# Weight maxima taken from the seventh attention piece on, and five planner durations set to traced values, in a one-core attention and softplus FFN kernel

## The chip, the cores and the metric

The kernel runs on 1 core of one Trainium2 chip. The metric is the device time of one execution in microseconds (us). The kernel before takes 1098.19 us, the median of 3 runs (1097.35 to 1099.35).

Engine names below: PE is the matmul engine (PEld its weight loads), DVE the vector engine, ACT the scalar engine, POOL the GpSimd engine, SP the engine whose queue issues nearly all DMAs. Each engine executes its own instructions strictly in the order in which the program lists them, and waits on semaphores for the others.

## The reference

```python
# attention: B, H, S, D = 8, 8, 576, 64
scores = (q @ k.T) / sqrt(D)
cum    = cumsum(log(clip(f, 1e-4, 1)))
scores = where(causal, -1e9, scores + cum[:, None] - cum[None, :])
attn   = exp(scores - max(scores)); attn /= sum(attn) + 1e-9
x      = (attn @ v), heads side by side: 4608 tokens x 512
# FFN: w_in 512 x 2048, w_out 2048 x 512
h   = x @ w_in
out = (max(h, 0) + log1p(exp(-|h|))) @ w_out
```

All inputs and the output are float32; the weights arrive as 64-bit words and are rebuilt to float32 on the core.

## The kernel before, in words

**Pieces of attention.** The attention work is a list of 70 jobs, called pieces below and numbered n = 0, 1, ...: two quads (n = 0, 1) and four pairs (n = 2 to 5), which do parts of four or two heads of the first batch; eight rests (n = 6 to 13) and eight mixed ones (n = 14 to 21, second batch), and then 48 whole heads of the other six batches. `nfirst` is 6 and `nstart` is 14. A piece consists of scores (PE, tiles named `s<n>_...`), row minima of the negated scores (DVE, line 1095), exponentials with row sums (ACT, line 1123), a transposition of the weights, the product with v (PE, tiles `o<n>_...`) and the write into `x` (the batch's attention output). In pieces up to n = 21 the transposition is done on PE into banks called `b<n>_...` (lines 1265 and 1268), with copies out by ACT or DVE. In the 48 whole heads the weights are split into two fp16 halves in the buffer `cross` (high part by ACT, POOL or DVE at line 256 or 258, low part by DVE at line 1190) and a DMA transposes them; the product with v (line 1400) is then written to `x` by an ACT pass (line 1420, `shift`) and a DVE pass that adds the low half (line 1424, `put`).

**FFN.** Blocks of tokens go through `h` (up product), softplus and `acc` (down product). Blocks 0 and 1 use the float32 weights (lines 1524 and 1645). From block 2 on all operands are fp16 high and low parts, scaled by powers of two (lines 1543 and 1626). For these scales the kernel needs the largest magnitude of each quarter of `w_in` and of the whole of `w_out`.

**Maxima of the weights.** `load_w_in` and `load_w_out` load one of 32 pieces of 128x512 (DMA `sti`, `sto`; then ACT, DVE, POOL, ACT and DVE passes that rebuild float32). Right behind the load each calls `largest`, which adds one reduction: DVE's line 564 for `w_in` (16 of them); for `w_out` either an ACT pass at line 562 or DVE's line 564. When a quarter's four maxima are listed, the main loop calls `find_top` at the next piece: a reduction on DVE (line 582, `tops`), a transposition on PE (line 586, tile `top<g>`, which needs a PSUM bank), a DVE reduction (589), a PE matmul (593) and five small DVE passes (598 to 602). `split_w_in` and `split_w_out`, which make the fp16 weights, wait for that.

**What sets the order.** Nothing is ordered by hand. Every step is an `Op` with one or more possible engines, each with a duration in us and a bias (`On(engine, cost, bias, port)`), the ops that it needs, and the buffers that it takes. `Plan.run` is a list scheduler over a window of 700 ops: it repeatedly takes the op that can start first by these durations, on the engine on which it would end first, and appends its instructions to that engine's list. So the durations decide both the order on each engine and which engine does a step. For each kind of buffer there is a queue in the order in which the ops were added, and an op that is not marked `loose` can take a buffer only when it is first in that queue. The PSUM banks of attention (tag `att`, at most four, later three) are one such kind: scores and `find_top`'s transposition are loose, the transposition of the weights (`weights`, tiles `b`) is not. `plan.fill` adds dummy matmuls on PE (`fill`, line 1823) where the plan leaves PE more than 0.5 us without work, about one per 0.215 us of 70% of the gap; it is switched off with the first down product.

Of the kernel before, what the change touches and what calls it, by code (L numbers as in the profile page):

```python
# [39 lines left out]

W_FROM, W_EACH = 0, 3
S_FROM, S_EACH = 9, 4


class Op:
# [220 lines left out]
def tile_decay_attention_softplus_ffn(  # L266
# [159 lines left out]
    h_up, h_down = (  # L426
        cpool.tile([P, len(BLOCKS), NG], F32, name=x) for x in ("h_up", "h_down")
    )
    tops_left = []
    top_ops, top_set, out_set = {g: [] for g in range(NG + 1)}, {}, []  # L430
    BITS = 0x7F800000

# [231 lines left out]
    def load_w_in(i):  # L664
        def new():
            w_in32[i] = piece("woh", i + 1)
            return w_in32[i]

        cc, fq = i % NCC, i // NCC
        src = w_in[cc * P : (cc + 1) * P, fq * 512 : (fq + 1) * 512]  # L670
        w_in_ready[i] = load_f64(src, new, f"i{i}")
        largest(i, 0, w_in32, on_dve(512))

    def load_w_out(i):
        def new():
            w_out32[i] = piece("wol", i + 1)
            return w_out32[i]

        w_out_ready[i] = load_f64(w_out[i * P : (i + 1) * P], new, f"o{i}")
        largest(i, 1, w_out32, [on_act(DM, 0.19), on_dve(DM, bias=SPARE_BIAS)])  # L680

    def split_w_in(i):
        cc, fq = i % NCC, i // NCC
# [199 lines left out]
    def attention(job):  # L883
# [139 lines left out]
        def prepare():  # L1023
            def begin(e):
                nonlocal t, tb, qA, qB, kA, kB
                t = T[number % 2]
                tb = t.bitcast(F32)
                qA, qB, kA, kB = (t[:, i, :] for i in range(4))

            def decay_rows(e):  # L1030
                e.dma_start(out=tb[64:ST, 1::2, :], in_=aug_d[bh])

            def q_hi(e):
                copy(e, t[:, 0, :], st["q"])

            def q_hi2(e):
                e.dma_start(out=tb[0:64, 1, :], in_=tb[0:64, 0, :])

            def q_lo(e):
                e.tensor_sub(t[64:P, 0, :], st["q"][64:P], tb[64:P, 0, :])  # L1040

            def k_hi(e):
                copy(e, t[:, 2, :], st["k"])

            def k_lo(e):
                e.tensor_sub(t[0:64, 3, :], st["k"][0:64], tb[0:64, 2, :])

            if not mixed_:
                split_v()
            if number < nplain + 2:  # L1050
                set_rows(number % 2, T0_end[2 * (number % 2)] + T0_end[2 * (number % 2) + 1])
            start = add(NO_ENGINE, begin, after=T_set[number % 2], takes=("T",), lag=0.0)
            a = add_dma(decay_rows, 18, after=[start, decay_ready["rows"]])
            lo_on = On("DVE", 0.75, 0.0, True)
            q1 = add(casts(S), q_hi, after=[start, st["qk"]])
            q2 = add(lo_on, q_lo, after=[q1])
            q3 = add_dma(q_hi2, 144, after=[q1])
            k1 = add(casts(S), k_hi, after=[start, st["qk"]])
            k2 = add(lo_on, k_lo, after=[k1])
            give("raw", [q2, k2])  # L1060
            st["T"] = [a, q2, q3, k2]


        def stat_tile(ti):
# [12 lines left out]
            for i, (a, z, acc) in enumerate(pieces):  # L1077
                box = {}
                final = z == end

                def scores(e, box=box, a=a, z=z):
                    o = keep_bank(box, "bank", "att", f"s{n}_{ti}_{a}")[:, 0 : z - a]
                    box["o"] = o[0:n_q]
                    if plain:
                        e.matmul(  # L1085
                            o, part32(0, q0, q0 + P), part32(1, a, z), start=True, stop=not quad,
                        )
                        return
                    o = box["o"]
                    e.matmul(o, qA[:, q0:end], kA[:, a:z], start=True, stop=False)  # L1090
                    e.matmul(o, qB[0:ST, q0:end], kB[0:ST, a:z], start=False, stop=True)  # L1091

                def row_min(e, box=box, w=z - a, i=i, final=final):
                    right = MW - P + n_q if final else w
                    e.tensor_tensor_reduce(  # L1095
                        out=box["o"], in0=box["o"], in1=cmask[0:n_q, right - w : right],
                        scale=-0.125, scalar=m0 if i else 3.0e38, op0=ALU.add, op1=ALU.min,
                        accum_out=m1 if final else m0,
                    )

                def sums(e, box=box, h=heads[ti % len(heads)]):
                    c, (plus, minus) = cum[0][:, 0:P], (x[:, h : h + 1].to_broadcast([BH, P]) for x in eye8)
                    e.matmul(box["o"], c, plus, start=False, stop=False)
                    e.matmul(box["o"], minus, c, start=False, stop=True)

                on = on_pe32(z - a) if plain else on_pe(z - a, 2)
                o = add(on, scores, after=st["T"], takes=("att",), loose=True)
                if quad:
                    o = add(on_pe32(2 * P), sums, after=[o, decay_ready["quad"]] + eye8_set)
                    cum_used.append(o)  # L1110
                m = add(
                    On("DVE", 0.076 + (z - a) / 960), row_min, lag=0.2, after=[o] + mask_set + stat_set,
                    takes=("stat",) if ti == 0 and i == 0 else (),
                )
                st.setdefault("scores", []).append(o)
                st.setdefault("min", []).append(m)
                mins.append(m)
                todo.append((a, z, acc, box))
# [47 lines left out]
        def turn_tile(ti):  # L1166
# [17 lines left out]
            for w, (to1, to2), of in todo:  # L1184

                def first_part(e, to1=to1, of=of):
                    times(e, to1, of, f_)

                def second_part(e, to1=to1, to2=to2, of=of):
                    e.scalar_tensor_tensor(to2, of, f_, to1, ALU.mult, ALU.subtract)  # L1190

                a = add(scales(w), first_part, after=deps)
                st["split"].append(
                    add(On("DVE", 0.12 + w / 960, 0.0, True), second_part, after=[a])
                )
            if ti < nt - 1:
                return
# [189 lines left out]
        def output(gi):  # L1387
# [37 lines left out]

            needs = last + x_taken.get(b, [])
            takes = () if b in x_taken else ("x32",)
            c = add(on_act(w, 0.095, psum=True), shift, after=needs, takes=takes)
            d = add(On("DVE", 0.136 + w / 960), put, after=[c])
            x_taken.setdefault(b, [c])  # L1430
            puts = [d]
            wrote.setdefault(b, []).append((tok, tok + w, d))
# [394 lines left out]
    for n in range(len(jobs) + 1):  # L1827
        while tops_left and tops_left[0][0] < n:
            find_top(tops_left.pop(0)[1])
        number_of["n"] = n  # L1830
        cur, nxt = att[n], att[n + 1]

        def prep(n=n, nxt=nxt):
# [40 lines left out]
            credit = run_ffn(credit + share)  # L1874
        old = cur
        if n >= nstart:
            while tops_left:
                find_top(tops_left.pop(0)[1])
            while splits_left:
                split_w_in(splits_left.pop(0)[0])  # L1880
            while out_splits:
                out_splits.pop(0)()
# [45 lines left out]
```

## Time and profile before

| | |
|---|---|
| median of 3 runs | 1098.19 us |
| the profiled execution itself | 1096.39 us |
| span in its trace | 1094.4 us |
| PE busy | 1047.5 us (96%) |
| DVE busy | 884.7 us (81%) |
| ACT busy | 833.1 us (76%) |
| POOL busy | 336.7 us (31%) |
| mean granted PE clock | 0.994 of full speed |

All shares and times of the profile belong to the one profiled execution, which is 1.80 us below the median. Times in the timelines count from the start of the span. "Busy" of PE includes the dummy `fill` matmuls. In the timelines each float32 matmul on PE shows as two records.

### The profile page before, as it was taken

To read this page: it belongs to the slowest core of one execution; us is meant where nothing else is said; L and a number is where in the kernel's file an instruction comes from. 1 tells how busy PE (TensorE), PEld (TensorE's weight loads), DVE (VectorE), ACT (ScalarE), POOL (GpSimd) and SP (SyncE) were. 2 spreads that over 40 slices of the span, in tenths; PEclk is the share of its full clock that TensorE was granted. 3 is DMA by queue.
4 is the path that set the end of the run, shared out by engine and by line. 5 is a ranking of instruction groups with operands and counts; after the bars stand their busy time and mean duration, and the time that the engine had idled before them with its cause. 6 is when DMAs were issued, how large, how long until landed. Compare 5 with 4: busy or idle time off the path is not lost.

```text
span 1094.4 us, 19162 instructions
## 1 busy us (share of the span) xinstructions
PE 1047.5 (96%) x6315; PEld 639.5 (58%) x6315; DVE 884.7 (81%) x2274; ACT 833.1 (76%) x2008; POOL 336.7 (31%) x431
## 2 busy tenths in 40 slices
PE   8999999989999999989999999989999999999998
PEld 7677777766556454556655544546655545456554
DVE  6899998899788998998788998888878998763332
ACT  5899899978778877878778777777787877655554
POOL 3234123334224542434243442342332343100000
PEclk9999999989999999999999999999999999999999
DMA  8777424447646665556555565555453654311000
GB/s 259 223 214 243 114 75 122 117 122 183 150 112 145 149 175 137 142 132 163 130 133 144 130 159 142 125 140 151 99 138 95 154 130 97 72 37 40 20 1 29
DMA packets 229299, 140.69 MB, mean 129 GB/s; under 512 B 191648, under 2 KB 208320, under 8 KB 229200
## 3 DMA queue, kind: packets, MB, share of 16 engines
q1 hardware_dynamic: 229032, 139.32, 50.4%
q8 instruction: 50, 0.82, 0.3%
q14 instruction: 49, 0.40, 0.1%
q10 hardware_dynamic: 168, 0.15, 0.0%
HBM read 73.27 MB, written 10.62 MB: 77 GB/s over the span
## 4 chain that ended last, share of the span: by engine, by line
PE 42%; DVE 32%; ACT 13%; issue 6%; POOL 4%; DMA 3%; SPq 0%; DVEq 0%; POOLq 0%; ACTq 0%
PE h L1543 14%; PE acc L1626 13%; DVE cross L1190 9%; ACT p L1123 6%; DVE s L1095 5%; DVE e L1589 4%; PE h L1524 2%; DVE x L1424 2%; DVE gh L1600 2%; POOL cross L258 2%; PE b L1265 2%; PE o L1321 2%; PE s L1090 2%; PE s L1085 2%; ACT gh L256 1%
## 5 line engine op out<-in xcount | busy, mean ns | idle before, releaser
L1543 PE MATMUL h<-xh,wi 128*128 128x256 f16 (+2 forms) x1536 | 375.7, 320 | 13.8 <-ACT p L1123 8.1
L1626 PE MATMUL acc<-wo,gh 128*128 128x512 f16 x1632 | 383.7, 381 | 0.3 <-ACT gh L256 0.2
L1543 PEld LDWEIGHTS <-wi 128*128 128x128 f16 x2304 | 213.9, 99 | 142.7 <-issue 22.5
L1123 ACT ACTIVATE p<-s,negm 128x288 f32<-128x288 f32 (+7 forms) x384 | 183.1, 479 | 96.7 <-DVE negm L1095 91.8
L1626 PEld LDWEIGHTS <-gh 128*128 128x128 f16 x1632 | 152.3, 98 | 169.6 <-issue 5.8
L1543 PE MATMUL h<-xl,wi 128*128 128x256 f16 (+2 forms) x768 | 233.1, 319 | 4.1 <-DVE xl L1498 4.1
L1589 DVE SCALAR_TENSOR_TENSOR e<-e,x 128x512 f32<-128x512 f32 (+1 forms) x152 | 98.8, 650 | 102.3 <-ACT e L1577 102.0
L1190 DVE SCALAR_TENSOR_TENSOR cross<-p,rsum,cross 128x512 f16<-128x512 f32 (+4 forms) x288 | 169.9, 621 | 11.1 <-POOL cross L258 7.9
L258 POOL TENSOR_SCALAR cross<-p,rsum 128x64 f16<-128x64 f32 (+4 forms) x158 | 155.5, 1001 | 34.9 <-DVE rsum L1143 17.7
L262 POOL CAST T<-raw 128x576 fp32r<-128x576 f32 x74 | 58.8, 808 | 332.6 <-PE s L1090 314.1
L256 ACT ACTIVATE gh<-e,g_up 128x512 f16<-128x512 f32 (+1 forms) x149 | 100.5, 675 | 75.8 <-DVE e L1589 74.5
L1095 DVE CUSTOM_DVE_ANT_0 s<-s,cmask 128x288 f32<-128x288 f32 (+6 forms) x320 | 136.4, 435 | 13.9 <-PE s L1091 6.7
L1090 PE MATMUL s<-T 128*64 128x64 f32 x336 | 128.9, 393 | 15.6 <-DVE x L1424 11.7
L1574 ACT ACTIVATE e<-h,h_down 128x512 f32<-128x512 f32 (+1 forms) x152 | 96.7, 636 | 49.1 <-PE h L1543 48.3
L1600 DVE SCALAR_TENSOR_TENSOR gh<-e,g_up,gh 128x512 f16<-128x512 f32 (+1 forms) x152 | 106.4, 700 | 30.3 <-ACT gh L256 28.5
L1091 PE MATMUL s<-T 68*64 68x64 f32 x336 | 97.9, 296 | 0.0
L1581 ACT ACTIVATE x<-h,h_down 128x512 f32<-128x512 f32 (+1 forms) x152 | 96.8, 637 | 0.1
L1577 ACT ACTIVATE e<-e 128x512 f32<-128x512 f32 (+1 forms) x160 | 93.6, 585 | 0.1
L1090 PEld LDWEIGHTS s<-T 128*64 128x64 f32 x336 | 61.1, 182 | 40.9 <-DVE x L1424 14.2
L1400 PE MATMUL o<-cross,v 128*128 128x64 f16 (+4 forms) x528 | 79.8, 285 | 3.0 <-DVE x L1424 1.6
L1400 PEld LDWEIGHTS <-v 128*128 128x128 f16 x528 | 50.4, 98 | 45.5 <-issue 2.3
L1123 ACT ACTIVATION_READ_ACCUMULATOR p<-s,negm 128x1 f32 (+1 forms) x384 | 74.8, 195 | 0.0
(152 smaller groups left out, 1342.3 us busy)
## 6 DMA issues: line engine op xcount, KB each, us to landing
raw<-in_qkT SPq DMA_DIRECT2D x112, 288.0 KB
vr<-in_vR SPq DMA_DIRECT2D x64, 160.0 KB
out<-ob SPq DMA_DIRECT2D x35, 256.0 KB
sti<-in_w_in SPq DMA_DIRECT2D x16, 512.0 KB
sto<-in_w_out SPq DMA_DIRECT2D x16, 512.0 KB
T<-T SPq DMA_DIRECT2D x56, 144.0 KB
vp<-in_vR SPq DMA_DIRECT2D x24, 320.0 KB
T<-in_qkT SPq DMA_DIRECT2D x8, 288.0 KB
```

The lines of the kernel that those rows point to most:

```text
L256: e.activation(out, in_, AF.Copy, scale=by)
L258: e.tensor_scalar(out, in_, by, None, ALU.mult)
L1090: e.matmul(o, qA[:, q0:end], kA[:, a:z], start=True, stop=False)
L1091: e.matmul(o, qB[0:ST, q0:end], kB[0:ST, a:z], start=False, stop=True)
L1095: e.tensor_tensor_reduce(out=box["o"], in0=box["o"], in1=cmask[0:n_q, right - w : right], scale=-0.125, scalar=m0 if i else 3.0e38, op0=AL ...
L1123: e.activation(o, box["o"], AF.Exp, bias=m1, scale=-1.0, accum_out=acc)
L1190: e.scalar_tensor_tensor(to2, of, f_, to1, ALU.mult, ALU.subtract)
L1400: e.matmul(box["ps"][:, w - x.shape[-1] : w], st["v16"][:, c], x, start=i == 0, stop=i == len(todo) - 1,)
L1543: e.matmul(o, l, r, start=m == 0, stop=m == 11)
L1589: e.scalar_tensor_tensor(o, box["e"], LARGE, x, ALU.min, ALU.max)
L1600: e.scalar_tensor_tensor(box["l"], box["e"], up, box["h"], ALU.mult, ALU.subtract)
L1626: e.matmul(st["acc", tt], l, r[fc], start=first and m == 0, stop=last and m == 2,)
```

## The change

Two things are changed.

First, `load_w_in` and `load_w_out` no longer add the maximum at once. They put it into one of two lists (`sizes_left`), with the number of the piece at which it was put there. The main loop takes up to three (`M_EACH`) from each list at every piece from n = 6 (`nfirst`) on, if they were put there at an earlier piece; at the end of piece 14 and later the lists are emptied.

Second, five durations by which the scheduler plans are changed: the low parts of q and k (0.75 to 0.79), the row minimum (0.076 to 0.12 beside its length, with its lag from 0.2 to 0.16), the low part of the attention weights (0.12 to 0.19), `shift` (0.095 to 0.2) and `put` (0.136 to 0.19). What is computed stays the same.

```diff
+M_EACH = 3
...
-        largest(i, 0, w_in32, on_dve(512))
+        sizes_left[0].append((number_of["n"], lambda: largest(i, 0, w_in32, on_dve(512))))
...
-        largest(i, 1, w_out32, [on_act(DM, 0.19), on_dve(DM, bias=SPARE_BIAS)])
+        on = [on_act(DM, 0.19), on_dve(DM, bias=SPARE_BIAS)]
+        sizes_left[1].append((number_of["n"], lambda: largest(i, 1, w_out32, on)))
...
-            lo_on = On("DVE", 0.75, 0.0, True)
+            lo_on = On("DVE", 0.79, 0.0, True)
...
-                    On("DVE", 0.076 + (z - a) / 960), row_min, lag=0.2, after=[o] + mask_set + stat_set,
+                    On("DVE", 0.12 + (z - a) / 960), row_min, lag=0.16, after=[o] + mask_set + stat_set,
...
-                    add(On("DVE", 0.12 + w / 960, 0.0, True), second_part, after=[a])
+                    add(On("DVE", 0.19 + w / 960, 0.0, True), second_part, after=[a])
...
-            c = add(on_act(w, 0.095, psum=True), shift, after=needs, takes=takes)
-            d = add(On("DVE", 0.136 + w / 960), put, after=[c])
+            c = add(on_act(w, 0.2, psum=True), shift, after=needs, takes=takes)
+            d = add(On("DVE", 0.19 + w / 960), put, after=[c])
...
         number_of["n"] = n
+        if n >= nfirst:
+            for x in sizes_left:
+                for _ in range(M_EACH):
+                    if x and x[0][0] < n:
+                        x.pop(0)[1]()
...
         if n >= nstart:
+            for x in sizes_left:
+                while x:
+                    x.pop(0)[1]()
```

Since the scheduler places every instruction anew, the lists of all engines differ. Line numbers in the changed kernel are 1 or 2 higher up to line 1830, and 10 higher at the end.

On PE at the start of the program, in the kernel before, behind the scores of the pairs (`s2`, `s3`): the dummy matmuls, the transposition of the first maxima (`top0`), and only then the transpositions of the first quad's weights (`b0`).

```order
L1085 MATMUL s2_0_0_247<-T00_72 128x256 [waits DMAHW1_49,DMAHW0_49,Activation_49]
L1085 MATMUL s2_1_256_251<-T00_72 128x256 [waits Activation_49]
L1085 MATMUL s3_0_0_255<-T00_72 128x256 [waits Activation_49]
L1823 MATMUL fill_317<-cmask_74 128x128 x36
L586 MATMUL top0_354<-ident_66,tops_104 1x128 [waits DVE_49,Activation_49]
L1823 MATMUL fill_317<-cmask_74 128x128 x5
L593 MATMUL top0_354<-ident_66,top_row_105 128x1 [waits DVE_49]
L1265 MATMUL b0_0_376<-ident_66,p0_640_95 128x128 [waits Activation_49]
L1265 MATMUL b0_0_376<-ident_66,p0_640_95 128x128
L1268 MATMUL b0_0_376<-ident_66,cross_102 128x128
```

The same place on PE in the changed kernel:

```order
L1087 MATMUL s2_0_0_247<-T00_72 128x256 [waits DMAHW1_49,DMAHW0_49,Activation_49]
L1267 MATMUL b0_0_251<-ident_66,p0_640_95 128x128 [waits Activation_49]
L1267 MATMUL b0_0_251<-ident_66,p0_640_95 128x128
L1270 MATMUL b0_0_251<-ident_66,cross_102 128x128 [waits Activation_49]
L1267 MATMUL b0_1_257<-ident_66,p0_640_95 128x128 x2
L1270 MATMUL b0_1_257<-ident_66,cross_102 128x128 [waits DVE_49]
L1087 MATMUL s2_1_256_262<-T00_72 128x256
L1087 MATMUL s3_0_0_272<-T00_72 128x256 [waits Activation_49]
L1323 MATMUL o0_275<-cross_102,vr0_163 64x128 [waits DMAHW3_49,Activation_49]
L1323 MATMUL o0_275<-cross_102,vr0_163 64x128
```

The first quad's `b0` now follows the first score of piece 2, and neither `top0` nor a `fill` stands ahead of it. In all, the list of PE holds 43 `fill` before and 17 now; `top0` moves from row 31 of PE's list to row 159, behind the first up products.

On DVE at the same time, before: the rebuilding of the first pieces of `w_in` (`ti`, `woh`) with a maximum behind each (`sizes_w`), and `tops` behind the fourth.

```order
L1143 RECIPROCAL rsum1_88<-lsum1_80 128x4 [waits DVE_49]
L631 TENSOR_SCALAR ti0_260<-ti0_260 128x512 [waits Activation_49]
L648 SCALAR_TENSOR_TENSOR woh1_dt_float32_262<-ti0_260,woh1_dt_float32_262 128x512 [waits Activation_49,Pool_49]
L631 TENSOR_SCALAR ti1_273<-ti1_273 128x512 [waits Activation_49]
L564 TENSOR_REDUCE sizes_w_103<-woh1_dt_float32_262 128x1 [waits DVE_49]
L631 TENSOR_SCALAR ti2_280<-ti2_280 128x512 [waits Activation_49]
L648 SCALAR_TENSOR_TENSOR woh2_dt_float32_271<-ti1_273,woh2_dt_float32_271 128x512 [waits Activation_49,Pool_49]
L564 TENSOR_REDUCE sizes_w_103<-woh2_dt_float32_271 128x1 [waits DVE_49]
```

And in the changed kernel, behind the first row minimum of piece 2:

```order
L1139 SCALAR_TENSOR_TENSOR lsum1_80<-lsum1_80,part1_84 128x4 [waits Activation_49]
L263 COPY cross_102<-b0_1_257 128x384 [waits PE_49]
L1145 RECIPROCAL rsum1_88<-lsum1_80 128x4 [waits DVE_49]
L1097 ISA s2_1_256_262,negm2_77<-s2_1_256_262,cmask_74 128x256 [waits PE_49]
L1097 ISA negm2_77 128x1
L632 TENSOR_SCALAR ti0_269<-ti0_269 128x512 [waits Activation_49]
L1097 ISA s3_0_0_272,negm3_78<-s3_0_0_272,cmask_74 128x256 [waits PE_49]
L1097 ISA negm3_78 128x1
L1361 TENSOR_TENSOR x32_0_291<-o0_275,cross_102 128x128 [waits PE_49]
```

Attention steps stand between the rebuilding passes, and the maxima of the first quarter come later (rows 72 to 76 of DVE's list, with `tops` at row 108 instead of 52).

In the part with whole heads the order changes in many small places. One of them on PE: the scores of the third tile of piece 56 (`s56_2`), which before stand right behind the last product of piece 54 (`o54_1`) and wait for DVE.

```order
L1400 MATMUL o54_1_8467<-cross_102,v16_54_8034 128x192
L1400 LDWEIGHTS v16_54_8034
L1400 MATMUL o54_1_8467<-cross_102,v16_54_8034 128x64
L1090 MATMUL s56_2_0_8483<-T0_1223 128x320 [waits DVE_49]
L1091 MATMUL s56_2_0_8483<-T0_1223 128x320
L1543 LDWEIGHTS wi16_0_390
L1543 MATMUL h9_0_8447<-xh9_7236,wi16_0_390 128x256
```

In the changed kernel the same scores stand ahead of both products of piece 54, and behind `o54_1` come scores that wait for ACT:

```order
L1092 MATMUL s56_2_0_8419<-T0_1177 128x320 [waits Activation_49]
L1093 MATMUL s56_2_0_8419<-T0_1177 128x320
L1545 LDWEIGHTS wi16_0_720
L1545 MATMUL h9_0_8423<-xh9_7249,wi16_0_720 128x256 [waits Activation_49]
```

```order
L1402 MATMUL o54_1_8471<-cross_102,v16_54_8036 128x192
L1402 LDWEIGHTS v16_54_8036
L1402 MATMUL o54_1_8471<-cross_102,v16_54_8036 128x64
L1092 MATMUL s56_3_0_8487<-T0_1177 128x448 [waits Activation_49]
L1093 MATMUL s56_3_0_8487<-T0_1177 128x448
```

Over the whole program 74 score matmuls of line 1090 wait for DVE before and 71 now; of these, 18 before and 16 now have no other matmul between themselves and the last product with v. Steps with a choice of engine move too: high parts of 128x512 attention weights on DVE 11 to 2, on ACT 46 to 45, on POOL 39 to 49; high parts of v on DVE 8 to 9, on ACT 25 to 11, on POOL 15 to 28; maxima of `w_out` on ACT 16 to 11, on DVE 0 to 5.

## Rows read from the trace of the kernel before

**Rows 1.** Stretches of the whole run: length, busy time of each engine, clock, DMA
```profile
0.00:60.00 60.00, 53.63 (x372) 41.59 (x373) 46.98 (x147) 43.96 (x116) 19.01 (x48) 1.00 0.80 227
60.00:120.00 60.00, 60.00 (x406) 44.88 (x404) 56.23 (x153) 55.02 (x136) 20.97 (x23) 1.00 0.72 220
120.00:180.00 60.00, 59.30 (x428) 44.03 (x427) 57.24 (x162) 54.98 (x146) 13.68 (x15) 1.00 0.39 103
180.00:240.00 60.00, 55.18 (x410) 41.08 (x409) 50.95 (x166) 50.72 (x146) 19.59 (x25) 0.94 0.49 122
...
sum 1094.40, PE 1047.52 PEld 639.49 DVE 884.71 ACT 833.13 POOL 336.75; mean PE 58.20 PEld 35.53 DVE 49.15 ACT 46.28 POOL 18.71
```

**Rows 2.** Timeline of PE, 13 to 48 us: start, length, instruction, idle before
```profile
13.75 8.20 PE L1823 MATMUL fill<-cmask 128*128 128x128 f32 x72
24.37 0.27 PE L586 MATMUL top<-ident,tops 128*1 128x128 f32 x1 [2.42 <-DVE tops L582]
24.48 1.28 PE L1823 MATMUL fill<-cmask 128*128 128x128 f32 x10
...
25.99 0.44 PE L1265 MATMUL b<-ident,p 128*128 128x128 f32 x2
...
26.70 0.61 PE L1823 MATMUL fill<-cmask 128*128 128x128 f32 x4
...
32.13 1.95 PE L1524 MATMUL h<-x,woh_dt_float 128*128 128x128 f32 x16
...
43.19 0.44 PE L1321 MATMUL o<-cross,vr 128*64 128x128 f32 x4 [1.28 <-ACT cross L262]
```

**Rows 3.** Timelines of ACT, DVE and SP, 11 to 30 us
```profile
11.87 0.28 ACT L262 COPY cross<-rsum 128x128 f32<-128x128 f32 x1
...
12.00 0.22 DVE L262 COPY cross<-rsum 128x128 f32<-128x128 f32 x1
...
22.62 0.69 DVE L648 SCALAR_TENSOR_TENSOR woh_dt_float<-ti,woh_dt_float 128x512 uint32<-128x512 uint32 x1
23.34 0.69 DVE L564 TENSOR_REDUCE sizes_w<-woh_dt_float 128x1 f32<-128x512 f32 x1
...
29.47 0.54 SPq L959 DMA_DIRECT2D T<-in_qkT  x1
```

**Rows 4.** Waits over the whole run: who for whom, us in total, times, longest
```profile
PE s L1090 <- DVE x L1424: 11.7, 13, 2.4
...
DVE cross L1190 <- POOL cross L258: 7.9, 19, 1.1
...
PE h L1543 <- DVE x L1424: 4.5, 6, 1.7
...
PE o L1400 <- DVE x L1424: 1.6, 1, 1.6
```

**Rows 5.** Timeline of PE at piece 56's scores
```profile
739.24 0.42 PE L1090 MATMUL s<-T 128*128 128x320 f32 x1 [2.38 <-DVE x L1424]
```

**Rows 6.** Groups by line and shape: busy us, mean ns of one, idle before
```profile
L1190 DVE SCALAR_TENSOR_TENSOR cross<-p,rsum,cross 128x512 f16<-128x512 f32 x96 | 70.7, 747 | 0.3
...
L258 POOL TENSOR_SCALAR cross<-p,rsum 128x512 f16<-128x512 f32 x39 | 62.2, 1598 | 0.0
...
L1424 DVE SCALAR_TENSOR_TENSOR x<-o,v_down,x 64x512 f32<-64x512 f32 x48 | 35.8, 745 | 1.2 <-ACT x L1420 0.4
...
L1190 DVE SCALAR_TENSOR_TENSOR cross<-p,rsum,cross 64x64 f16<-64x64 f32 x48 | 32.4, 674 | 7.1 <-POOL cross L258 6.0 <-ACT cross L256 0.8
...
L258 POOL TENSOR_SCALAR v<-vr,v_up 128x320 f16<-128x320 f32 x15 | 21.9, 1462 | 10.2 <-PE o L1400 6.2 <-PE o L1321 3.7 <-DMA raw<-in_qkT 0.2
...
L1190 DVE SCALAR_TENSOR_TENSOR cross<-p,rsum,cross 128x64 f16<-128x64 f32 x48 | 16.7, 347 | 0.1
...
L564 DVE TENSOR_REDUCE sizes_w<-woh_dt_float 128x1 f32<-128x512 f32 x16 | 10.7, 675 | 0.1
...
L258 DVE TENSOR_SCALAR cross<-p,rsum 128x512 f16<-128x512 f32 x11 | 7.3, 666 | 0.1
```

More of the change, by code (lines that the diff above doesn't have):

```diff
@@ L428, in tile_decay_attention_softplus_ffn @@
     )
-    tops_left = []
+    tops_left, sizes_left = [], ([], [])
     top_ops, top_set, out_set = {g: [] for g in range(NG + 1)}, {}, []
```

## The prediction

> **What bounds the kernel now.** I read the table of stretches first. PE works 1047.5 of 1094.4 us, so at most 46.9 us of idle time can be had, and what is worth reading is where it lies [rows 1]. The first stretch of 60 us lacks 6.4 us, the next two together 0.7 us, the fourth 4.8 us, at a clock of 0.94. From 60 to 180 us PE is the bound, with DVE close behind (113.5 of 120 us). Later each stretch lacks a few us.
>
> Busy is not the same as useful: the timeline of PE shows dummy matmuls from 13.75 us on, 8.20 + 1.28 + 0.61 = 10.09 us of them, 86 records, so 43 matmuls of 0.235 us. Behind the first group PE stands for 2.42 us until DVE has the maxima of the first quarter of `w_in`, and only then, at 25.99 us, come the transpositions of the first quad [rows 2]. Their inputs had long been there: the copies of the row sums that they read end at 12.2 us [rows 3]. So from 13.75 to 25.99 us PE does nothing but two tiny matmuls of `top0`. The cause is the queue for attention's banks, in the planner: the transposition of the maxima was listed ahead of `b0`, takes a bank of the same kind, and `b0` isn't loose, so it could not be planned before it. The maxima in turn wait for four weights to land and be rebuilt, until 23.3 us and 0.69 us more for the last maximum [rows 3].
>
> In the part with whole heads, PE's own waits are for `put`, which frees a bank or finishes x: 11.7 + 4.5 + 1.6 = 17.8 us, 20 times [rows 4]. The one at 739.24 us is typical, 2.38 us in front of scores that stand right behind a product with v [rows 5].
>
> **The change part by part.** (a) The start. `top0` no longer stands in front of `b0`, since the maxima are listed only from piece 6 on. 26 of 43 dummy matmuls go, 26 x 0.235 = 6.1 us, and the wait of 2.42 us goes: 8.5 us [rows 2]. A second limit gives the same: the next thing that must come from memory is the first up product, at 32.13 us, and its last weight was rebuilt at 23.3 us, 8.8 us before [rows 2, 3]. What is late next are the copies out of `b`, which now come on DVE and ACT between rebuilding passes. The nearest row is the 1.28 us that a product with v waits for such a copy at 43.19 us [rows 2]. Four products with v now stand ahead of the first up product, so 0 to 5.1 us are given back; I take 1.5 us, near one such wait, since by the list there are other matmuls between most `b` and their `o`. Net -7.0 us, between -8.5 and -3.4 us. SP's queue moves along: its load at 29.47 us waited for a buffer that the scores of piece 3 free, and they now stand ahead of the first up product [rows 3].
>
> (b) What was taken out comes back later. 16 maxima of 0.675 us on DVE stay 16 [rows 6]; eight of them stood in the first 60 us; in DVE's list now four stand at rows 72 to 76 and the others from row 109 on, so up to 4 x 0.675 = 2.7 us move into the stretch up to 180 us. Five maxima of `w_out` go from ACT to DVE there, 3.4 us at the same duration. Together 6.1 us come to a stretch in which DVE has 6.5 us free [rows 1]. What hides them is that room, and that the fp16 weights aren't used before the float32 blocks are through. I take 0, with 6.1 us if the cover is gone. The loads come earlier by as much as PE does: 227 x 60 + 220 x 60 is 26.8 MB in 120 us, in 113 us it would be 237 GB/s. The DMA engines are busy 0.80 and 0.72 there [rows 1], so I count nothing.
>
> (c) The durations. `put` of 512 columns takes 0.745 us [rows 6] where the plan had 0.136 + 0.533 = 0.669 and now has 0.723; the low part of 512 takes 0.747 where it had 0.653 and has 0.723 [rows 6]. With the plan's DVE later, it puts other work where PE would wait. The lists show a small effect: of scores that wait for DVE, 18 stood with nothing between themselves and the product with v, and 16 do now. Of 17.8 us I take 2/18, -2.0 us [rows 4]; the bounds are 0 and one half, -8.9 us, if every such place becomes milder like the one of piece 56, which goes altogether.
>
> (d) The engines. Ten more high parts of 512 columns go to POOL, at 1.598 us instead of 0.666 on DVE, 0.93 us later each; DVE already waits 7.9 us for such parts [rows 4, 6]. By the share of 10 to 39 it is 2.0 us of DVE waits; a quarter of it on PE makes +0.5 us. The bounds are 0 and 9.3 us, each of the ten in full. The 13 more parts of v on POOL, 1.462 us each, are needed only at the product with v, about a piece later: 0 as long as POOL is busy a third of the time.
>
> Sum against the profiled execution: 1096.39 - 7.0 + 0 - 2.0 + 0.5 = 1087.9 us. The median of the runs lies 1.80 us above it, so 1089.7 us.
>
> A rule that speaks against (d): the low part of 64x64 takes 0.674 us on DVE where that of 128x64, with as many elements a row, takes 0.347 [rows 6]. The Trainium skill (SBUF — State Buffer, "Who interferes with whom") says that DVE and GpSimd share a pair of ports under an exclusive lock, so that a DVE pass with two SBUF inputs and a GpSimd pass block each other in full. These rows fit it, as one of these passes follows POOL's and the other mostly doesn't; by it all of POOL's added time would stop DVE, which is the second rival.
>
> **The rivals.** *Given back by 180 us.* DVE is nearly full from 60 to 180 us, and if the 6.1 us of (b) don't fit, or the loads hold the start back, PE's lead of 7.0 us melts to 0.9. With (c) and (d) at nothing that is 1096.39 - 0.9 + 1.8 = 1097.3 us. For it speaks DVE's 113.5 of 120 us, against it that PE, not DVE, was without a gap there [rows 1].
>
> *Slower: POOL holds DVE.* POOL gets 10 x 1.598 + 13 x 1.462 = 35.0 us of passes more, less what narrower ones leave it [rows 6]. If they hold DVE's passes, and with them `put` and the row minima, and a third of that reaches PE, 11.7 us come on top of (a): 1096.39 - 7.0 + 11.7 + 1.8 = 1102.9 us. It decides from 9.2 us on, a good quarter. For it: DVE waits for POOL 19 times; against it: the longest is 1.1 us, and DVE's own list gets shorter by 13 rows.
>
> *A better plan throughout.* If the waits for `put` halve, the sum is 1096.39 - 7.0 - 8.9 + 0.5 + 1.8 = 1082.8 us; with no new waits at the start 1081.3. For it: the durations corrected are those of just the passes that PE waits for. Against it: 16 of 18 places remain.
>
> *No effect.* The gap at the start reappears somewhere before the weights: 1098 us. Against it: the list itself has lost the 26 matmuls.
>
> **How the numbers follow.** Chances: the forecast 0.62, given back 0.15, slower by POOL 0.10, the better plan 0.10, no effect 0.03. The forecast's own range is 1081 to 1096 us, from the ends of (a) and (c) and 2 us of (d). The range 1079 to 1099 us takes in the first rival and the better plan and leaves out the slower one. A difference under 0.2%, 2.2 us, can't be told from none. Faster by more: 0.62 + 0.10 + 0.03 of the given-back case, 0.75. Within: 0.10 of that case and no effect, 0.13. Slower: 0.10 + 0.02, 0.12.
>
> **What would show it.** Right on (a): the first `b` at 13 us instead of 25.99, the first up product at about 24 us, and dummy matmuls of about 4 us in all. Wrong on (a): waits for copies of over 5 us before 60 us, or a clock below 1.00 in the first stretch. On (b): the stretches from 60 to 180 us should lack no more than 1 or 2 us of PE; over 5 us is the first rival. On (c): PE's waits for `put` at 14 to 18 us. On (d): DVE's wait for POOL's high parts at 8 to 11 us; over 15 us, with waits for `put` over 25 us, is the slower rival. The forecast is wrong as a whole if PE's idle time after 240 us changes by more than 8 us either way.

## The result, and the profile after

The changed kernel takes 1068.99 us, the median of 4 runs (1068.78 to 1069.77), against 1097.77 us (1097.18 to 1099.35) for the kernel before beside it: a ratio of 0.974, 95% interval 0.9725 to 0.9756. The profiled execution took 1069.17 us with a span of 1067.1 us. The gain of 28.8 us is more than three times the forecast, and the time lies 10 us below the range.

The stretches of the changed kernel, in the columns of [rows 1], with a fifth one up to 1050 us:

```profile
0.00:60.00 60.00, 55.77 (x380) 41.61 (x380) 48.08 (x153) 45.43 (x122) 19.93 (x48) 1.00 0.87 251
60.00:120.00 60.00, 58.23 (x361) 42.51 (x362) 55.67 (x144) 51.29 (x125) 18.18 (x23) 0.94 0.65 191
120.00:180.00 60.00, 59.50 (x423) 44.11 (x422) 58.07 (x165) 54.22 (x147) 17.55 (x15) 1.00 0.39 104
180.00:240.00 60.00, 54.51 (x396) 41.06 (x395) 52.27 (x170) 50.90 (x147) 16.97 (x24) 0.91 0.50 125
240.00:1050.00 810.00, 799.72 (x4643) 461.25 (x4642) 650.89 (x1626) 624.58 (x1455) 290.20 (x332) 1.00 0.50 123
```

The last stretch in the kernel before, which [rows 1] hold only in their sum:

```profile
240.00:1050.00 810.00, 779.01 (x4497) 447.54 (x4497) 661.08 (x1627) 606.61 (x1427) 263.50 (x321) 1.00 0.51 123
```

The first 240 us gain nothing: PE lacks 4.2 + 1.8 + 0.5 + 5.5 = 12.0 us where it lacked 11.9. From 240 to 1050 us it lacks 10.3 us where it lacked 31.0. That is 20.7 us of the 27.3 us of span, all in the part with whole heads, for which the forecast had 2.

The start on PE in the changed kernel, in the columns of [rows 2]:

```profile
13.21 0.38 PE L1267 MATMUL b<-ident,p 128*128 128x128 f32 x2
...
21.24 1.73 PE L1825 MATMUL fill<-cmask 128*128 128x128 f32 x14
...
24.47 3.84 PE L1526 MATMUL h<-x,woh_dt_float 128*128 128x128 f32 x32
...
61.64 1.26 PE L1087 MATMUL s<-T 66*128 66x320 f32 x2 [1.98 <-issue]
```

The first `b` comes at 13.21 us instead of 25.99 and the first up product at 24.47 instead of 32.13; dummy matmuls fall from 10.1 to 4.6 us. The scores of piece 8 start 9.9 us earlier than before. Those of piece 10 are 3.1 us ahead, those of piece 20 are 0.5 us late, and those of piece 32 0.6 us late; at piece 56 they are 13.9 us ahead and at piece 69 23.1.

PE's and DVE's waits in the changed kernel, which answer to [rows 4]:

```profile
PE h L1545 <- DVE x L1426: 3.7, 4, 1.8
PE s L1092 <- ACT p L1125: 3.4, 4, 1.7
PE h L1545 <- DVE xl L1500: 2.8, 3, 1.8
...
DVE cross L1192 <- POOL cross L259: 4.6, 11, 0.7
```

The wait of scores for `put`, 11.7 us in 13 places, is gone, that of products with v too, and that of `h` is 3.7 us instead of 4.5: 17.8 us became 3.7. DVE waits less for POOL's high parts, not more.

The place of [rows 5], piece 56, in the changed kernel's timelines, first PE:

```profile
719.41 0.49 PE L1092 MATMUL s<-T 128*128 128x320 f32 x1
...
721.22 0.22 PE L1402 MATMUL o<-cross,v 128*128 128x64 f16 x2
...
722.59 1.44 PE L1402 MATMUL o<-cross,v 128*128 128x512 f16 x9
723.86 0.45 PE L1092 MATMUL s<-T 128*128 128x448 f32 x1
```

and DVE:

```profile
722.88 0.28 DVE L1426 SCALAR_TENSOR_TENSOR x<-o,v_down,x 64x64 f32<-64x64 f32 x1
```

`put` starts 1.44 us after the end of the product that it follows (721.44 us), where the kernel before took 5.90 us (733.02 to 738.92, shown below). And the scores of 320 columns are through before that, so PE goes on without a gap.

Groups by shape of the changed kernel, against [rows 6]:

```profile
L1192 DVE SCALAR_TENSOR_TENSOR cross<-p,rsum,cross 128x512 f16<-128x512 f32 x96 | 70.9, 753 | 1.1 <-POOL cross L259 0.8
...
L259 POOL TENSOR_SCALAR cross<-p,rsum 128x512 f16<-128x512 f32 x49 | 82.0, 1675 | 0.0
...
L259 POOL TENSOR_SCALAR v<-vr,v_up 128x320 f16<-128x320 f32 x28 | 46.3, 1652 | 29.5 <-PE o L1402 28.0 <-PE o L1323 1.1 <-DMA raw<-in_qkT 0.4
```

### The profile page after: what moved, and what is told of

The parts are those of the page before. It is cut to its first block, busy times and chain, and to the rows that moved or that the text cites. A ratio compares the mean times of both kernels' runs of the same rounds, so it can differ in the third digit from the quotient of the medians.

```text
span 1067.1 us, 19053 instructions
## 1 busy us (share of the span) xinstructions
PE 1040.8 (98%) x6263; PEld 636.5 (60%) x6263; DVE 869.0 (81%) x2262; ACT 833.6 (78%) x2005; POOL 362.8 (34%) x441
## 4 chain that ended last, share of the span: by engine, by line
PE 66%; DVE 17%; ACT 6%; issue 4%; POOL 4%; DMA 2%; DVEq 0%; POOLq 0%; ACTq 0%
PE h L1545 24%; PE acc L1628 23%; PE o L1402 4%; DVE s L1097 3%; PE s L1092 3%; DVE cross L1192 3%; PE s L1093 2%; ACT p L1125 2%; PE h L1526 2%; DMA cross<-cross 2%; PE b L1267 2%; PE acc L1647 2%; POOL cross L259 2%; DVE e L1591 2%; PE s L1087 1%
## 5 line engine op out<-in xcount | busy, mean ns | idle before, releaser
L259 POOL TENSOR_SCALAR cross<-p,rsum 64x64 f16<-64x64 f32 (+4 forms) x157 | 164.1, 1061 | 36.2 <-DVE rsum L1145 15.1
L1192 DVE SCALAR_TENSOR_TENSOR cross<-p,rsum,cross 128x512 f16<-128x512 f32 (+4 forms) x288 | 161.7, 596 | 6.9 <-POOL cross L259 4.6
L263 POOL CAST T<-raw 128x576 fp32r<-128x576 f32 x73 | 53.6, 747 | 267.5 <-PE s L1092 228.5
L257 ACT ACTIVATE gh<-e,g_up 128x512 f16<-128x512 f32 (+1 forms) x144 | 97.0, 674 | 56.6 <-DVE e L1591 55.6
L1602 DVE SCALAR_TENSOR_TENSOR gh<-e,g_up,gh 128x512 f16<-128x512 f32 (+1 forms) x152 | 109.4, 719 | 30.2 <-ACT gh L257 29.4
```

What stands on the lines that cost most here:

```text
L259: e.tensor_scalar(out, in_, by, None, ALU.mult)
L1602: e.scalar_tensor_tensor(box["l"], box["e"], up, box["h"], ALU.mult, ALU.subtract)
```

## The experiments

Each run's time has beside it its ratio to the kernel before on the same chip, with the 95% interval. "Idle" is what PE lacks from 240 to 1050 us in the run's trace.

**Which half of the change.** e1 has the five durations alone, e2 the deferred maxima alone.

```diff
# e1: the five durations of the change; sizes_left and M_EACH are left as before
# e2: the change, with
-            d = add(On("DVE", 0.19 + w / 960), put, after=[c])
+            d = add(On("DVE", 0.136 + w / 960), put, after=[c])
# ... and the other four durations as before
```

> The kernel before with the five durations of the change, the maxima taken as pieces arrive. Theory D (the durations do it in the part with whole heads: PE's waits for `put` go because the plan no longer believes DVE to be free early): 1070 to 1078 us, PE's waits for `put` under 6 us in all, the start as before (first `b` at about 26 us). Theory M (the deferred maxima do it, by a head start that lasts): 1092 to 1098 us. Theory R (any new plan can fall this way): nothing said, somewhere from 1065 to 1100 us.

> The change with the five durations as before: only the maxima are deferred. Theory D: 1093 to 1098 us; the lead of about 10 us at 50 us is given back by 230 us, as in the changed kernel, and PE's waits for `put` stay at 14 to 18 us. Theory M: 1070 to 1080 us. Theory R: anywhere from 1065 to 1100 us, with the difference spread over the whole run.

e1: 1071.86 us (0.9782, 0.9744 to 0.982), idle 8.9 us. e2: 1096.25 us (0.9988, 0.9973 to 1.0004), idle 33.8 us. From piece 44 on every head of e1's trace starts within 0.7 us of the changed kernel's. (That execution took 1069.47 us; e1's four runs fall into two pairs, near 1069 us at a mean clock of 0.995 and near 1075 us at 0.990.) The durations make the gain; the deferral alone makes no difference that can be measured, though it too is 12.4 us ahead at piece 8.

**Which durations.** e3 changes the two passes that PE waits for by name, e4 the other three.

```diff
# e3
+            c = add(on_act(w, 0.2, psum=True), shift, after=needs, takes=takes)
+            d = add(On("DVE", 0.19 + w / 960), put, after=[c])
# e4
+            lo_on = On("DVE", 0.79, 0.0, True)
+                    On("DVE", 0.12 + (z - a) / 960), row_min, lag=0.16, ...
+                    add(On("DVE", 0.19 + w / 960, 0.0, True), second_part, after=[a])
```

> The kernel before with only `shift` (0.095 to 0.2) and `put` (0.136 to 0.19). Theory D, if what counts is the passes that PE waits for: 1072 to 1082 us, most of the gain, and waits for `put` under 6 us. If the gain is that of the sum of DVE's work in the plan (theory D'): under a third of it, 1090 us or more. Theory R: no relation to the run with all five.

> The kernel before with only the low parts of q and k (0.75 to 0.79), the row minimum (0.076 to 0.12, lag 0.2 to 0.16) and the low part of the attention weights (0.12 to 0.19). Theory D, by the passes that PE waits for: 1088 to 1097 us, waits for `put` 10 to 18 us. Theory D' (DVE's whole work in the plan: 48 heads with about ten low parts and ten minima each, against one or two `put`): 1075 to 1082 us. Theory R: no relation.

e3: 1095.46 us (0.9981, 0.9957 to 1.0005), idle 29.5. e4: 1080.21 us (0.9849, 0.9824 to 0.9874), idle 15.3. Theory D, by the passes that PE waits for, fell; D', by DVE's whole work in the plan, holds so far (17 us of 25). The waits say it in one line each, e3 first, then e4:

```profile
PE s L1090 <- DVE x L1424: 14.2, 14, 2.4
```

```profile
PE s L1090 <- DVE x L1424: 0.9, 1, 0.9
```

With `put` itself planned right, PE waits longer for it than before; with `put` planned as before and three other passes changed, the scores' wait is down to 0.9 us. Why, the timeline of the kernel before shows, ahead of the wait of [rows 5]. The product on PE:

```profile
732.80 0.22 PE L1400 MATMUL o<-cross,v 128*128 128x64 f16 x2
```

DVE:

```profile
733.43 1.01 DVE L1498 SCALAR_TENSOR_TENSOR xl<-x,x_up,xh 128x768 f16<-128x768 f32 x1
734.78 0.49 DVE L1190 SCALAR_TENSOR_TENSOR cross<-p,rsum,cross 64x64 f16<-64x64 f32 x1 [0.34 <-POOL cross L258]
735.20 0.60 DVE L258 TENSOR_SCALAR xh<-x,x_up 128x768 f16<-128x768 f32 x1
736.09 1.41 DVE L1190 SCALAR_TENSOR_TENSOR cross<-p,rsum,cross 128x256 f16<-128x256 f32 x2 [0.28 <-POOL cross L258]
737.42 1.58 DVE L1498 SCALAR_TENSOR_TENSOR xl<-x,x_up,xh 128x768 f16<-128x768 f32 x1
738.92 0.27 DVE L1424 SCALAR_TENSOR_TENSOR x<-o,v_down,x 64x64 f32<-64x64 f32 x1
739.12 0.35 DVE L1095 CUSTOM_DVE_ANT_0 s<-s,cmask 128x192 f32<-128x192 f32 x1
```

and ACT at the same time:

```profile
735.75 0.31 ACT L1420 ACTIVATE x<-o,v_down 64x64 f32<-64x64 f32 x1
```

The product ends at 733.02 us. ACT comes to `shift` 2.73 us later. The input of `put` is then ready at 736.06 us and `put` runs at 738.92, for 0.27 us. In between DVE works through a queue. The row minimum behind it is later still: its scores ended at 733.3 us. `put` is only the pass at which the lateness reaches PE.

**One duration at a time.**

```diff
# e5 (row minimum alone)
+                    On("DVE", 0.12 + (z - a) / 960), row_min, lag=0.16, ...
# e6 (low part of the weights alone)
+                    add(On("DVE", 0.19 + w / 960, 0.0, True), second_part, after=[a])
# e10 (low parts of q and k alone)
+            lo_on = On("DVE", 0.79, 0.0, True)
```

> The kernel before with only the row minimum changed (0.076 to 0.12, lag 0.2 to 0.16). The three durations of the run before gave 17 us. Theory B (DVE is backlogged because the plan gives too little time to the passes ahead of `put`; each edit counts by what it adds to DVE's planned time per head, 7 x 0.044 = 0.31 us for the minima, 6 x 0.07 = 0.42 us for the low parts of the weights, 0.08 for those of q and k): 7 us, 1088 to 1093 us, waits for `put` near 10 us. Theory E (what helps is which engine takes the high parts, not the times): by its lists, which give POOL more of them, 1080 to 1085 us. Theory R (any new plan can fall this way): no relation.

> The kernel before with only the low part of the attention weights (0.12 to 0.19). Theory B: 9 us, 1085 to 1091 us, waits for `put` under 10 us; with the row minimum alone the two gains add up to about 17 us. Theory E: as for the row minimum, near 1082 us, since POOL's share of the high parts rises as much. Theory R: no relation.

> The kernel before with only the low parts of q and k (0.75 to 0.79, twice a head, so 0.08 us a head, a quarter of what the row minimum adds). Theory B in proportion: 3 to 5 us of gain, 1092 to 1096 us. Theory R: 1075 to 1090 us, as with the row minimum or the low part of the weights alone, since the size of the edit plays no role.

e5: 1083.04 us (0.987, 0.9846 to 0.9894), idle 26.6. e6: 1082.15 us (0.9864, 0.9833 to 0.9896), idle 21.5. e10: 1088.40 us (0.9914, 0.9886 to 0.9943), idle 22.2. Each gains, but not in proportion: 0.08 us a head gives 9 us, 0.26 us (there are six minima, not seven) 16, and the three together only 17. Both e5 and e6 gain more than theory B gave them (B: each edit counts by what it adds to DVE's planned time) and lie where theory E had them (E: what helps is which engine takes the high parts). But e5 leaves that choice nearly as it was, with 12 high parts of 512 columns on DVE instead of 11 and 37 on POOL instead of 39; e7 below tests E by itself. The time of e10 lies in the range that theory R (luck of a new plan) gave. And e5 gains by another way in part: its trace has no stretch at half clock up to the last 0.3 us, where that of before has 13.6 us, and its fourth stretch lacks 1.6 us instead of 4.8.

**Controls: the engines alone, twice the step, next to no step, the other way.**

```diff
# e7 (before)
-SCALE_BIAS = 1.0
+SCALE_BIAS = 2.0
-COPY_BIAS = 0.1
+COPY_BIAS = 0.6
# e8 (changed kernel): 0.83; 0.164 with lag 0.12; 0.26; 0.305; 0.244
# e9 (before)
-            r = add(On("DVE", 0.19), over, after=[r], lag=0.25)
+            r = add(On("DVE", 0.195), over, after=[r], lag=0.25)
# e11 (before): 0.71; 0.032 with lag 0.24; 0.05; 0.0; 0.082
```

> The kernel before, all durations as before, with the scheduler's bias against DVE raised for the high parts of the weights (1.0 to 2.0) and for copies and the high part of x (0.1 to 0.6), so that DVE's share of these passes falls as far as in the changed kernel. Theory E: 1075 to 1085 us. Theory B: the passes that DVE keeps are still planned too short, so the waits for `put` stay above 10 us: 1090 to 1100 us.

> The changed kernel with each of the five durations moved by the same step again (low parts of q and k 0.83, row minimum 0.164 with lag 0.12, low part of the weights 0.26, `shift` 0.305, `put` 0.244). Theory B with times that are now right: too much time planned, DVE's idle time rises and PE waits for softplus or scores instead: 1070 to 1080 us. Theory B with times that are still too short (the low parts of 64 columns take 0.35 to 0.67 us where the changed plan has 0.257): another gain, 1058 to 1067 us. Theory R: no relation.

> The kernel before with one duration moved by next to nothing (the reciprocal of the row sums, 0.19 to 0.195 us, once a head): the plan falls anew from the part with whole heads on, but for no reason of DVE's time. Theory B (DVE's planned time is too short, and longer times gain until the plan has room): 1094 to 1101 us. Theory R (any new plan can fall this way, the kernel before has an unlucky one): 1075 to 1090 us.

> The kernel before with the five durations moved the other way by the same steps or nearly (low parts of q and k 0.71, row minimum 0.032 with lag 0.24, low part of the weights 0.05, `shift` 0, `put` 0.082). Theory B: slower than before, 1105 to 1125 us, with more of PE's time waiting for DVE. Theory R: as likely faster as slower, 1080 to 1100 us.

e7: 1091.25 us (0.9955, 0.9924 to 0.9985), idle 28.5: DVE keeps none of the 11 high parts of 512 columns and its busy time falls by 7.7 us, and that is worth 1.6 to 8.3 us by the interval, not the 13 to 23 that theory E gave it. e8: 1072.35 us (0.9773, 0.9747 to 0.9799), idle 11.4: no more to be had. e9: 1100.01 us (1.0017, 0.9999 to 1.0034), idle 33.4: a new order for no reason gains nothing. e11: 1110.68 us (1.0128, 1.0095 to 1.0161), idle 41.5. So the sign follows DVE's planned time, and theory R fell as the cause, though it may lie behind the uneven sizes: e10 and e3 add 0.08 and 0.11 us a head and gain 9.2 and 1.8 us.

| run | DVE time added to the plan, us a head | against before, us | idle, us |
|---|---|---|---|
| e11 | -0.87 | +13.1 | 41.5 |
| before | 0 | | 31.0 |
| e9 | 0.005 | +2.4 | 33.4 |
| e10 | 0.08 | -9.2 | 22.2 |
| e3 | 0.11 | -1.8 | 29.5 |
| e5 | 0.26 | -15.7 | 26.6 |
| e6 | 0.42 | -16.5 | 21.5 |
| e4 | 0.76 | -17.0 | 15.3 |
| e1 | 0.87 | -25.4 | 8.9 |
| e8 (with the deferral) | 1.74 | -26.4 | 11.4 |

(A head has two low parts of q and k, six minima, six low parts of the weights and two `put`.)

**The low part by its real widths**, in the changed kernel:

```diff
-                    add(On("DVE", 0.19 + w / 960, 0.0, True), second_part, after=[a])
+                    add(On("DVE", (0.65 if n_q == w else 0.3 + 0.00078 * w), 0.0, True), second_part, after=[a])
```

> The changed kernel with the low part of the attention weights planned as the trace has it by width: 0.3 + 0.00078 us an element, and 0.65 us for the 64x64 part (changed plan: 0.19 + w/960, so 0.257 for both parts of 64 columns). It adds 0.7 us a head to DVE's planned time. Theory B: 1062 to 1069 us, a small gain, PE's waits for DVE under 5 us; if the room is already enough, 1068 to 1073. Theory R: no relation, 1060 to 1085 us.

e12: 1074.59 us (0.9784, 0.9764 to 0.9804), idle 13.2: a miss, outside both ranges of theory B. (It adds 0.5 us a head, not 0.7.) Truer numbers for one pass gain nothing once there is room.

**The old order with a faster DVE.** If the old order is bad only because DVE is slower than planned, it must be good when DVE is made faster. e14 is the kernel before and e15 the changed one, each with its lists in the same order; from piece 24 on the low part of the weights covers half its columns.

```diff
-                    e.scalar_tensor_tensor(to2, of, f_, to1, ALU.mult, ALU.subtract)
+                    x = slice(0, of.shape[-1] // (2 if number > 23 else 1))
+                    e.scalar_tensor_tensor(to2[..., x], of[..., x], f_, to1[..., x], ALU.mult, ALU.subtract)
```

> The kernel before, the same instructions in the same order on every engine, but from piece 24 on the low part of the attention weights covers half the columns (the other half is left out), some 0.9 us less of DVE's time a head, about what the durations of the change add to the plan. Theory B (the old order is made for a DVE that is faster than the real one): 1070 to 1082 us, PE's idle time after 240 us 10 to 18 us instead of 31. Theory O (the old order is bad by itself, whatever DVE takes): 1092 to 1099 us.

> The changed kernel with the same halved low parts (the other half left out), the order again the same. Theory B: the plan already has the time, so little is left to gain: 1062 to 1068 us. Theory O, or simply a kernel bound by DVE: as much gain as in the kernel before, or 1050 to 1060 us.

e14: 1072.03 us (0.9767, 0.9753 to 0.9782). e15: 1055.84 us (0.9617, 0.9599 to 0.9636). Their last stretches, e14 first:

```profile
240.00:1050.00 810.00, 795.17 (x4620) 458.23 (x4619) 628.61 (x1639) 618.32 (x1450) 253.50 (x320) 1.00 0.51 123
```

```profile
240.00:1050.00 810.00, 804.24 (x4671) 463.25 (x4669) 614.39 (x1627) 628.47 (x1462) 272.95 (x330) 1.00 0.51 123
```

The same 38 to 39 us of DVE's busy time are worth 25 us (idle 31.0 to 14.8) in the old order and 13 us (10.3 to 5.8, and less time at half clock) in the new one. So theory O fell: the old order is nearly as fast as the changed kernel when DVE is as fast as the plan had it. But 13 us in e15 is more than theory B alone allowed; DVE's real time counts too. By e15's 13 us for 38, the 13.3 us that e1 takes off DVE's busy time are worth some 4 to 5 us of its 25; by e14's 25 us for 39, 8 to 9 (both estimates). The rest, 16 to 21 us, is the order.

**Where the head start goes.** e13 is the changed kernel with the maxima over 64 of 512 columns (the others are left out), the lists in the same order; e16 has the maxima of `w_out` on ACT alone; e17 is the changed kernel again; e18 is e16 with e7's biases.

```diff
# e13
+                e.tensor_reduce(at, x[i][:, 0:64], AX.X, ALU.max, apply_absolute_value=True)
# e16
-        on = [on_act(DM, 0.19), on_dve(DM, bias=SPARE_BIAS)]
+        on = on_act(DM, 0.19)
# e18: both lines of e7 and that of e16
```

> The changed kernel, the same instructions in the same order on every engine, but each maximum of a weight piece covers 64 of its 512 columns (what it leaves out: the other columns of the maxima), so that 21 passes of 0.67 us on DVE fall to about 0.2, some 10 us of DVE's time between 24 and 118 us. Theory V (the lead of the start is lost because DVE is full from 60 to 180 us): 3 to 8 us of it stay, 1061 to 1067 us, and piece 20 starts 3 us or more earlier than in the changed kernel. Theory S (it is lost in the one stall near 60 us and the low clock behind it, and in later waits that DVE does not cause): 1067 to 1071 us.

> The changed kernel with the maxima of `w_out` on ACT alone (five of sixteen stand on DVE). Theory S: the stall of 2 us near 61 us and the 6.8 us at half clock go, 1063 to 1066 us. Theory V: 3.4 us less on DVE, which ACT (54 of 60 us) must take: 1066 to 1070 us.

> The changed kernel itself, unchanged. Theory C (the PE clock falls near 62 us in some executions of it and not in others, and that alone is 3 to 4 us): two groups of times, near 1065 and near 1069 us, with the higher clock in the faster ones. If the fall belongs to this order of instructions: 1068 to 1070 us in all.

> The changed kernel with the maxima of `w_out` on ACT alone, as in e16, and the bias against DVE raised for the high parts (1.0 to 2.0) and copies (0.1 to 0.6), as in e7. Theory B with room enough (PE's idle time after 240 us is 9 us, so little is left): 1061 to 1067 us. If DVE's real time still decides, as the 13 us of e15 suggest: 1056 to 1061 us. If POOL's longer passes now come on the path: 1067 to 1075 us.

e13: 1065.14 us (0.9704, 0.9686 to 0.9722). e16: 1064.21 us (0.97, 0.9683 to 0.9716). e17: 1068.61 us (0.9721, 0.9696 to 0.9747). e18: 1070.03 us (0.9736, 0.9705 to 0.9767). The stretches behind 60 us of the changed kernel, and then of e15, which has the same instructions there in the same order:

```profile
60.00:62.00 2.00, 0.36 (x1) 0.36 (x2) 1.91 (x5) 1.80 (x3) 0.00 (x0) 0.95 0.63 137
62.00:64.00 2.00, 1.87 (x6) 0.97 (x5) 1.97 (x7) 1.71 (x7) 0.00 (x0) 0.50 0.86 293
...
66.00:68.00 2.00, 2.00 (x11) 2.00 (x11) 0.83 (x1) 1.91 (x4) 1.84 (x3) 0.50 1.05 279
```

```profile
60.00:62.00 2.00, 0.98 (x3) 0.50 (x4) 1.93 (x5) 1.79 (x5) 0.07 (x1) 1.00 0.75 181
62.00:64.00 2.00, 2.00 (x19) 2.00 (x19) 1.97 (x8) 2.00 (x7) 0.25 (x1) 1.00 1.02 395
...
66.00:68.00 2.00, 2.00 (x14) 1.47 (x13) 2.00 (x6) 1.49 (x3) 1.17 (x3) 1.00 0.95 151
```

In the changed kernel PE stands for 1.98 us (the profile names nothing that it waits for: `issue` in the line at 61.64 us above), and its clock then falls to 1.2 GHz for 6.8 us. In e15 it stands for 1.56 and 0.62 us, as long in all, and the clock stays at 2.4 GHz. Piece 24 starts 3.6 us earlier in e15 than in the changed kernel, of which 0.8 us were there at 57 us already, and 4.5 us earlier in e13. So the nine tenths of a microsecond between these two are all that 21 maxima of 0.21 us instead of 0.67 seem to be worth. The time of e13 and its lead of 4.5 us at piece 20 are what theory V (DVE is too full for the maxima) expected, but e15 has 3.5 us of that lead with the maxima whole: V fell for the most part. That shorter maxima help PE to escape the fall of the clock is not excluded. In e16 the clock stays up there and PE lacks 0.8 us from 60 to 120 us instead of 1.8. Theory C had two groups for e17; three of its runs are near 1068.8 us (clock 0.990 to 0.991) and one at 1067.26 us (0.994), so in the changed kernel the fall is the rule. Why the traced execution of e15, with the same lists there, escaped it, the runs do not show. e16 is the fastest kernel that computes everything: 1063.3 to 1066.7 us in its runs against 1067.3 to 1069.8 us in eight of the changed kernel, though the two ran on different chips. In e18 the gain of e16 is gone again: PE's waits for `put` before `h` take 4.8 us after 240 us where e16 has 1.6. That POOL's longer passes are behind it, as one expectation had it, is not shown.

## Why the prediction was wrong

(a) The start was right as far as the step went: the places on PE came where the prediction has them, the first stretch kept its clock, no copy held PE for long, and at piece 8 the lead was 9.9 us. That it would last was wrong; the course is that of the first rival. Its cause is for the most part not the rival's, which had DVE too full for the maxima (e13 against e15). Up to 240 us the changed kernel saves 5.5 us of dummy matmuls and 2.1 us of PE's idle time in the first stretch. It loses 2.3 us of idle time in the next three (1.8 - 0.2 + 0.7) and 5.1 us by the clock, which is low for 6.8 us at 61.8 and for 10.2 us at 229.0 instead of 6.8 us at 231.7, at half speed each. 7.6 gained and 7.4 lost: term (a) is worth nothing here, not 7.0, and most of what takes it back is the clock, which the prediction considered in the first stretch alone.

(b) The 6.1 us that DVE was to hide did not matter. DVE worked 113.7 us of the 120 up to 180 us, where it had worked 113.5, and PE lacked 2.3 us there, a little over the 1 or 2 that the prediction allowed.

(c) This is the step that failed: "Of 17.8 us I take 2/18", with a bound of one half. The five durations gave 25.4 us in e1. Three things in it were wrong. It counted places on PE's list where scores stand right behind a product with v, of which 16 remain; but whether such a place waits depends on how late DVE is there. It took the wait's name for its cause: e3 shows that the duration of `put` is worth next to nothing, e4 that the minima and low parts, which nobody seems to wait for, carry most of it. And it bounded the term by the waits for `put` alone, though PE also waits for ACT's exponentials, and these wait for DVE's minima in their turn. PE's wait and then ACT's, before:

```profile
PE h L1543 <- ACT p L1123: 8.1, 9, 1.7
...
ACT p L1123 <- DVE negm L1095: 91.8, 118, 2.6
```

and in the changed kernel:

```profile
PE h L1545 <- ACT p L1125: 0.6, 2, 0.4
...
ACT p L1125 <- DVE negm L1097: 59.6, 97, 1.9
```

The rival "a better plan throughout" had the right course at half its size (15.4 us of gain in all; 28.8 came). The forecast's own sign of being wrong as a whole, PE's idle time after 240 us changed by more than 8 us, came true with 20.7. That the durations corrected add 0.87 us a head, 42 us over 48 heads, to a DVE that the plan took to have that time free, stood in the diff, and no step summed it.

(d) Ten more wide high parts and 13 more of v did go to POOL. DVE's wait for them fell from 7.9 to 4.6 us instead of rising to 8 to 11, and the rival that POOL holds DVE is excluded here: POOL's passes grew (1598 to 1675 ns, and 1462 to 1652 for v) while DVE's low part of 512 columns stayed (747 and 753 ns). The Trainium skill (SBUF — State Buffer, "Who interferes with whom") says that in a contest for the shared ports the one that issues first holds them and the other waits; these rows agree with POOL being the one that waits. So does e15: with the same lists and DVE's low parts halved, POOL's parts of v take 1336 ns instead of 1652 and its high parts of 512 columns 1636 instead of 1675.

Between the sum of the parts and the 27.3 us of span some 5 us stay open: the idle time after 240 us explains 20.7, the clock there 1.7 (3.4 us at half speed instead of 6.8). What also stays open is why 0.04 us on the low parts of q and k does as much as it does.

## What to carry to other kernels

A wait named in a profile is the place where lateness shows, not its source: look at the queue ahead of the pass that is waited for, and ask how long its input had been ready. When a list scheduler plans an in-order engine too fast, the error to sum is that of all its passes per round, not that of the pass waited for; here planned time doubled beyond the correction cost some 3 us (e8), while too little cost 13 (e11). The gains do not add up in proportion, so such a sum gives the sign and the order of size, not the microseconds. And an experiment with the lists unchanged and one engine made faster (e14) tells a bad order from a slow engine.

## What the runs showed of the hardware

The same instructions in the same order ran at either clock: two runs of e15 took 1053.4 and 1054.6 us at a mean clock of 0.996, two 1057.1 and 1057.3 us at 0.992, some 3 us apart. Near 60 us a stall of 1.98 us in the changed kernel, and one of 1.87 us in e17, were followed by 6.8 us at 1.2 GHz, and stalls of 1.56 and 0.62 us in e15 by none; what decides it, these runs do not show. The Trainium skill (TensorE: Matmul & The Clock Gate, Part 1) says of the first rise of the clock that its moment varies from run to run. The traces fit that: the six `warm` matmuls at the start, which stand alike in all four lists and begin at 2.32 or 2.33 us, took 4.85 us in the changed kernel and in e17, 4.43 us in e15 and 4.02 us in e13.

The low part of 64 rows by 64 elements took 674 ns on DVE before, 574 ns in the changed kernel, and 651 ns in e14 with half its elements: so most of that time does not go by the elements.
